# Batch 0 scored in float32 from raw q and k, and every tile of softmax weights split into two float16 halves and transposed by DMA

## The chip, the cores and the metric

The kernel runs on one core of a Trainium2 chip. The metric is the device time of one execution in microseconds, the median over runs. Engines are named as the profile names them: PE is TensorE (PEld its weight loads), DVE VectorE, ACT ScalarE, POOL GpSimd, SP the engine whose queue issues every DMA here.

## The reference

Three parts follow each other. The first is attention with a hash mask: 2 batches, 8 heads, 768 positions, head dimension 64.

```python
q_bits = (q @ proj > 0); k_bits = (k @ proj > 0)      # proj: 64 x 6
mask = bucket(q_bits)[..., :, None] == bucket(k_bits)[..., None, :]
scores = np.where(mask, (q @ k.T) / 8, -1e9)
attn = np.exp(scores - scores.max(-1, keepdims=True))
x = (attn / (attn.sum(-1, keepdims=True) + 1e-9)) @ v
```

Then `x` (1536 tokens x 512) passes a feed-forward layer with softplus, `(max(h,0) + log1p(exp(-|h|))) @ w_out` with `h = x @ w_in` (512 to 2048 to 512), and a gated layer, `(silu(x @ w_gate) * (x @ w_val)) @ w_out2` (512 to 1536 to 512). The feed-forward weights arrive as 64-bit floats and are turned into 32-bit ones, and then into pairs of 16-bit ones, on the chip.

## The kernel before

Precision comes from pairs: a float32 operand is scaled by a power of two, rounded to float16 (`hi`), and the remainder is kept as a second float16 (`lo`). A product of two such operands takes two or three float16 matmuls.

The work is cut into four chunks: batch 0 first half and second half of the query rows, batch 1 first and second half. A chunk has 8 heads of 3 tiles of 128 query rows each, so 24 tiles; a tile is a row block of 128 queries against all 768 keys. For each head the kernel loads k, v, q (`load_kv`, `load_q`), sums their squares and turns the sums into powers of two (`scales`), splits q and k into `natq` and `natk`, transposes these by DMA into `q` and `k` (`query_side`, `key_side`), copies the high half to the other 64 partitions, and lets `planes` make the mask rows: matmuls with the projection give the hash signs, which are written as plus or minus a large constant into rows 0 to 63 of the second operand. So each tile's score is four float16 matmuls of 384 columns (`qk`, L776), in which a mask mismatch comes out as a huge negative number. v is split in `value_side`.

In `units_of` a tile then runs: `qk` on PE; `mx` on DVE (L787), which copies the scores to SBUF, clamps them and takes the row maximum, and a second small DVE instruction (L792) that turns the maximum into the bias of the exponential; `ex` on ACT (L797). From there the kind of the tile decides. Kind F (the 24 tiles of the first half of batch 0): six PE transposes in float32 (L831), an ACT or DVE copy of the result to SBUF (L862), and six float32 matmuls with raw v (L870). Kind D (the other 72 tiles): a high half on ACT, POOL or DVE (L804, L812), a low half on POOL or DVE (L817), one DMA transpose of both (L823), and 18 float16 matmuls with the split v (L854). After the third tile the sums are inverted and the head's output is scaled into `xn`; after eight heads `x_tile` splits and transposes a chunk's rows into `xy`, and `ffn1` and later `ffn2` run on it.

The order of all instructions on all engines is written by a planner (`Order`) while the kernel is built: each step has an urgency, one or more ways (engine, cost, function, and a handicap in us from `BV`), and rings of buffers. Among the steps that can start earliest on an engine, the one of lowest urgency is taken; among ways, the one with the earliest end plus handicap. The engines then run their instructions in that order. Rings that matter here: `E` 3, `P` 2, `PT` 2, `z` (PSUM) 2, `f` (PSUM) 2, `k` 5, `q` 3. All DMAs go through SP's queue in order.

```python
KINDS = ("FFF", "DDD", "DDD", "DDD")          # kinds of a chunk's three tiles
s = ways(u + U["lo"], [("G", gps(S) + 0.05, lo(nc.gpsimd)), ("W", dve(S), lo(nc.vector), BV["lo"])], [s], uses=[E, P])
s = step(u, "D", (1.72, 1.9), tr, [s], takes=[PT], uses=[P], line="tr")
```

The order of visits: batch 0 first halves of heads 0 to 7, then second halves (k of three heads is loaded and split again, because the ring holds five), then batch 1. Beside batch 0 the 16 pieces of the first feed-forward layer's weights are converted on DVE, ACT and POOL (L394 to L448); beside the second half of batch 0 `ffn1` of chunk 0 starts. The gate weights wait until attention has left its buffers.

Of the kernel before, what the change touches and what calls it, by code (L numbers as in the profile page):

```python
# [31 lines left out]

class Step:
# [17 lines left out]
class Order:  # L51
# [8 lines left out]
    SLACK = 0.1077  # L60
# [123 lines left out]
def tile_hash_attention__softplus_ffn__silu_glu(  # L184
# [54 lines left out]
    BV = dict(tf=1.0, th=1.091, hi=2.161, lo=0.772, slo=0.117, wlo=-0.43, bits=0.477, meas=0.564, cv=-0.593, ca=0.872)  # L239
    U = dict(vl=0, tp=-2.89, th=-2, tl=-2, w2=53.21, qp=-7.63, kp=-4.93, kv=3.56, f1=0, y=40, ev=-9.89, ex=3.56, hi=-7.89, lo=2.67, gw=423.98, x=2.84)  # L240
# [22 lines left out]
    KINDS = ("FFF", "DDD", "DDD", "DDD")  # L263
    SPLIT = 3
    RINGS = {
# [41 lines left out]
    nc.vector.memset(ones, 1.0)  # L307

# [10 lines left out]
    nc.vector.tensor_scalar_mul(half_amp, amp, 0.5)  # L319
    floors = small(3)  # L320
# [8 lines left out]
    ones_mat = const.tile([128, 128], F32, name="ones_mat")  # L329
    nc.vector.memset(ones_mat, 1.0)  # L330
# [179 lines left out]
    praw = const.tile([128, NB], F32, name="praw")  # L510

    pm = small()

    def load_proj():
        for r in range(2):
            nc.sync.dma_start(out=praw[64 * r:64 * r + 64], in_=proj)
        for i in range(2):
            for w in range(2):
                nc.gpsimd.memset(pj[i][w], 0.0)

    def prep_proj():
# [12 lines left out]
        for w in range(2):  # L534
            nc.vector.tensor_copy(pj[1][w][:, 0:32], pj[0][w][:, 32:64])
            nc.vector.tensor_copy(pj[1][w][:, 32:64], pj[0][w][:, 0:32])

# [28 lines left out]
    def planes(u, i, n, src, dst, after, takes, uses):  # L566

        ps = [Slot("f") for _ in range(n)]

        def products(x, f):  # L570
            def go():
                new(ps_f, [128, 512], F32, f)
                for w in (1, 0):
# [9 lines left out]
        def bits(x, f):  # L583
            def go():
                nc.vector.tensor_scalar(
                    dst()[0:64, x * HS:(x + 1) * HS], f.t[0:64, 0:HS], thr[0:64, i:i + 1],
                    amp[0:64, i:i + 1], op0=ALU.is_gt, op1=ALU.mult,
                )
            return go

        def signs(x, f):
            def go():
                new(att, [64, HS], F16, hb[x])
                nc.scalar.activation(hb[x].t, f.t[0:64, 0:HS], AF.Sign, bias=low[0:64, i:i + 1])
            return go

        def offset(x):
            def go():
                nc.gpsimd.tensor_scalar(
                    dst()[0:64, x * HS:(x + 1) * HS], hb[x].t, half_amp[0:64, i:i + 1],  # L600
                    half_amp[0:64, i:i + 1], op0=ALU.mult, op1=ALU.add,
# [7 lines left out]
        for x, f in enumerate(ps):  # L609
            s = step(u, "E", pe(2 * HS), products(x, f), after, takes=[f], uses=uses)  # L610
# [25 lines left out]
    def scales(b, h, u, kv, ld_kv, qr, ld_q):  # L636
# [20 lines left out]
        def inverse():  # L657
            for i, c in enumerate((QK_SC, -QK_SC)):
                nc.vector.tensor_scalar(
                    inv[:, i:i + 1], e[:, 0:1], e[:, 1:2], c, op0=ALU.mult, op1=ALU.mult  # L660
                )
        ms = [
            ways(u, [("A", act(n) + 0.15, measure_a(i)), ("V", stt(n) - 0.07, measure_v(i), BV["meas"])],
# [10 lines left out]
    def key_side(b, h, u, hs, raw, ld, proj_ready):  # L674
# [28 lines left out]
        cp = ways(u, [("W", dve(NT * 128, 4), copy_v, BV["cv"]), ("A", act(NT * 128), copy_a, BV["ca"]),  # L703
# [4 lines left out]
    def value_side(u, hs, raw, ld, after=()):  # L708
# [9 lines left out]
        return dict(v=vs, v_ready=split(u, NT * D, parts, [g], [raw, vs]))  # L718

    def query_side(b, h, half, u, hs, raw, ld, proj_ready):  # L720
# [28 lines left out]
        cp = ways(u, [("W", dve(CN, 4), copy_v, BV["cv"]), ("A", act(CN), copy_a, BV["ca"]),  # L749
# [9 lines left out]
    def units_of(b, h, half, due, hs, kd, qd):  # L759

        c = 2 * b + half
        kinds = KINDS[c]
# [4 lines left out]
        for t in range(HT):  # L767
# [3 lines left out]
            def qk(t=t, z=z):  # L771
                a = new(ps_z, [128, 2, 512], F32, z)
                ts = slice(t * 128, (t + 1) * 128)
                for w in range(2):
# [6 lines left out]
            def mx(t=t, z=z, st=st, E=E):  # L781


                if t == 0:
                    new(att, [128, 2, HT], F32, sums)
                a = new(att, [128, 4], F32, st)
                nc.vector.tensor_scalar(  # L787
# [87 lines left out]
            s = step(u, "E", pe(4 * HS), qk, kd["ready"] + qd["ready"], takes=[z], uses=[kd["k"], qd["q"]],  # L875
# [469 lines left out]
```

## Time and profile before

| | us |
|---|---|
| median of 3 runs | 885.31 (883.08 to 885.72) |
| the profiled execution | 884.34 |
| span in its profile | 882.5 |
| PE busy | 779.3 (88%) |
| DVE busy | 584.9 (66%) |
| ACT busy | 460.3 (52%) |
| POOL busy | 407.7 (46%) |
| mean granted clock of PE | 0.957 |

The span is the time from the first to the last instruction of the profiled execution; 1.8 us of its time lie around it. A PE that is shown busy is not a PE at its peak, since matmuls overlap each other.

### The profile page before, as it was taken

The page shows a single profiled execution, that of the slowest core. Times are in us where ns is not written, and L with a number is a line of the kernel's source. Part 1 is how long each engine was busy: PE and PEld are TensorE (multiplying, and loading weights), DVE is VectorE, ACT ScalarE, POOL GpSimd, SP SyncE. Part 2 cuts the span into 40 slices and gives each one's busy share as a digit, 9 for nine tenths or more (in the row PEclk, how much of TensorE's full clock was granted, in tenths as well). Part 3 has the DMA queues.
Part 4 walks back from the last instruction along what each step waited for, and adds up shares of the span by engine and source line. Part 5 has one row for each costly group of instructions (what it writes and reads, how often), then busy time and mean ns, then how long its engine had stood idle before and what let it go on. Part 6 is the DMA issues. An engine that isn't in the chain of part 4 may idle for free.

```text
span 882.5 us, 14634 instructions
## 1 busy us (share of the span) xinstructions
PE 779.3 (88%) x5462; PEld 505.3 (57%) x5462; DVE 584.9 (66%) x1157; ACT 460.3 (52%) x847; POOL 407.7 (46%) x430
## 2 busy tenths in 40 slices
PE   3787776877889886779999999899999999999998
PEld 1565654444445553445566666555576676677666
DVE  4798888789989899999667799968911311220320
ACT  4666667668567688767568548624411211211220
POOL 2345346877578788877348418512311210210220
PEclk9988998889879998899999999999999999999999
DMA  6445457946668787857793541342200000000000
GB/s 186 124 146 167 112 131 172 189 100 149 117 135 162 159 139 146 151 98 135 120 157 70 185 161 40 127 160 96 96 12 25 1 9 28 1 1 36 1 1 36
DMA packets 195048, 90.05 MB, mean 102 GB/s; under 512 B 156640, under 2 KB 181664, under 8 KB 194976
## 3 DMA queue, kind: packets, MB, share of 16 engines
q1 hardware_dynamic: 194976, 89.11, 43.0%
q8 instruction: 43, 0.70, 0.3%
q14 instruction: 29, 0.24, 0.1%
HBM read 47.35 MB, written 3.15 MB: 57 GB/s over the span
## 4 chain that ended last, share of the span: by engine, by line
PE 49%; DVE 22%; DMA 10%; POOL 7%; issue 6%; ACT 3%; SPq 1%; DVEq 0%; POOLq 0%; ACTq 0%
PE z L1020 8%; PE z L1022 8%; PE z L1021 8%; DMA PT<-P 4%; PE f L1183 4%; PE f L1181 4%; PE f L1182 4%; DVE E L787 3%; DVE fr L1061 2%; DMA q<-natq 2%; POOL P L817 2%; DVE fr L1049 2%; PE z L776 2%; DVE w32b L399 1%; PE y L1020 1%
## 5 line engine op out<-in xcount | busy, mean ns | idle before, releaser
L1149 DVE SCALAR_TENSOR_TENSOR sg<-z,smalls,sg 128x384 f32<-128x384 f32 x96 | 59.2, 616 | 176.9 <-ACT sg L1143 175.4
L1158 POOL TENSOR_TENSOR sT<-sg,sT 128x384 fp32r<-128x384 f32 x48 | 51.8, 1080 | 217.0 <-ACT sT L1155 211.1
L797 ACT ACTIVATE E<-E,st,smalls 128x768 f32<-128x768 f32 x96 | 98.1, 1022 | 28.0 <-DVE st L792 25.8
L776 PE MATMUL z<-k,q 128*128 128x384 f16 x384 | 87.6, 359 | 15.7 <-DVE E L787 15.4
L787 DVE TENSOR_SCALAR_CACHE_REDUCE E<-z 128x768 f32<-128x768 f32 x96 | 91.2, 950 | 9.4 <-POOL P L817 5.3
L817 POOL TENSOR_TENSOR P<-E,P 128x768 f16<-128x768 f32 x51 | 87.0, 1708 | 12.7 <-ACT P L804 9.8
L1075 POOL TENSOR_TENSOR g<-fr,g 128x384 f16<-128x384 f32 x64 | 73.6, 1154 | 16.7 <-ACT g L1066 13.1
L1020 PE MATMUL f<-xy,w1h 128*128 128x384 f16 x192 | 65.8, 343 | 10.7 <-DVE fr L1049 9.1
L854 PE MATMUL pv<-v,PT 128*128 128x64 f16 x1296 | 52.4, 197 | 19.1 <-DMA PT<-P 18.4
L854 PEld LDWEIGHTS <-PT 128*128 128x128 f16 x1296 | 47.6, 101 | 34.5 <-DMA PT<-P 27.4
L1021 PE MATMUL f<-xy,w1h 128*128 128x384 f16 x192 | 65.6, 342 | 0.0
L1022 PE MATMUL f<-xy,w1l 128*128 128x384 f16 x192 | 65.4, 341 | 0.0
L1020 PE MATMUL z<-xy,wgh 128*128 128x384 f16 x192 | 62.6, 326 | 0.7 <-DVE sg L1149 0.7
L1020 PE MATMUL z<-xy,wvh 128*128 128x384 f16 x192 | 62.6, 326 | 0.0
L1021 PE MATMUL z<-xy,wvh 128*128 128x384 f16 x192 | 62.6, 326 | 0.0
L1022 PE MATMUL z<-xy,wvl 128*128 128x384 f16 x192 | 62.6, 326 | 0.0
L1022 PE MATMUL z<-xy,wgl 128*128 128x384 f16 x192 | 62.6, 326 | 0.0
L1021 PE MATMUL z<-xy,wgh 128*128 128x384 f16 x192 | 62.6, 326 | 0.0
L776 PEld LDWEIGHTS <-q 128*128 128x128 f16 x384 | 36.3, 106 | 45.5 <-issue 24.5
L1143 ACT ACTIVATE sg<-z,smalls 128x384 f32<-128x384 f32 x48 | 27.8, 580 | 63.6 <-PE z L1022 63.5
L1061 DVE SCALAR_TENSOR_TENSOR fr<-fa,smalls,fr 128x384 f32<-128x384 f32 x64 | 55.4, 869 | 7.8 <-ACT fa L1058 5.4
L1155 ACT ACTIVATE sT<-sg 128x384 fp32r<-128x384 f32 x48 | 25.1, 522 | 61.8 <-DVE sg L1149 61.6
(189 smaller groups left out, 2032.0 us busy)
## 6 DMA issues: line engine op xcount, KB each, us to landing
raw64a<-in_moe_w_in_dram SPq DMA_DIRECT2D x16, 512.0 KB, 4.6
raw64a<-in_moe_w_out_dram SPq DMA_DIRECT2D x16, 512.0 KB, 5.0
raw64b<-in_moe_w_gate_dram SPq DMA_DIRECT2D x12, 512.0 KB, 4.3
raw64b<-in_moe_w_val_dram SPq DMA_DIRECT2D x12, 512.0 KB, 4.9
raw64b<-in_moe_w_out_dram SPq DMA_DIRECT2D x12, 512.0 KB, 4.3
rawk<-in_k_dram SPq DMA_DIRECT2D x19, 192.0 KB, 2.7
rawv<-in_v_dram SPq DMA_DIRECT2D x19, 192.0 KB, 3.3
rawq<-in_q_dram SPq DMA_DIRECT2D x16, 192.0 KB, 3.0
```

What stands on the lines that cost most here:

```text
L776: nc.tensor.matmul(a[:, x, 0:HS], lhsT=qd["q"].t[:, w, ts], rhs=kd["k"].t[:, w, x * HS:(x + 1) * HS], start=(w == 0), stop=(w == 1),)
L787: nc.vector.tensor_scalar(new(att, [128, 2, HS], F32, E), z.t[:, :, 0:HS], MASK_FLOOR, None, op0=ALU.max, op1=ALU.max, accum_out=a[:, 0:1],)
L797: nc.scalar.activation(E.t, E.t, AF.Exp, bias=st.t[:, 1:2], scale=hs["inv"][:, 0:1], accum_out=sums.t[:, 0, t:t + 1],)
L817: return lambda: eng.tensor_tensor(P.t[:, 1, :], E.t.rearrange("p a b -> p (a b)"), P.t[:, 0, :], op=ALU.subtract)
L854: nc.tensor.matmul(pv.t[:, t, :], lhsT=PT.t[:, w, kk, :], rhs=values.t[:, kk, c0:c0 + D], start=(kk == 0 and w == 0 and c0 == 0), stop=(kk ...
L1020: nc.tensor.matmul(ps, lhsT=wh, rhs=xh, start=first, stop=False)
L1021: nc.tensor.matmul(ps, lhsT=wh, rhs=xl, start=False, stop=False)
L1022: nc.tensor.matmul(ps, lhsT=wl, rhs=xh, start=False, stop=last)
L1061: nc.vector.scalar_tensor_tensor(out=fr.t, in0=fa.t, scalar=sc[b]["sg"], in1=fr.t, op0=ALU.mult, op1=ALU.add)
L1075: return lambda: eng.tensor_tensor(g.t[:, 1], fr.t, g.t[:, 0], op=ALU.subtract)
L1149: return lambda: nc.vector.scalar_tensor_tensor(out=sg.t, in0=z.t[:, j, 0:CN], scalar=gvs[b, "gv"[j]][:, gi:gi + 1], in1=sg.t, op0=ALU.mul ...
L1158: return lambda: eng.tensor_tensor(sT.t[:, 1, :], sg.t, sT.t[:, 0, :].bitcast(F32), op=ALU.subtract)
```

## The change

All four chunks become kind D, so the PE transposes, the copies and the float32 products with v of the first half go, and its weights are split and transposed by DMA as the others are; v of batch 0 is split for both halves. In batch 0 (`PLAIN`), q and k are no longer measured, split or DMA-transposed: PE transposes them in float32 (`key_plain`, `query_plain`), ACT or DVE copies the result out of PSUM, `planes` uses one float32 matmul where it used two float16 ones, and writes its rows as float32 into partitions 64 to 127. A score tile is then two float32 matmuls (`qk`), `mx` takes a minimum of the negated score, which is the exponential's bias as it stands, so L792 goes there. In batch 1, L792 may run on ACT as well, and the ReLU of `ffn1` too. The planner's handicaps, urgencies and pacing numbers are new throughout.

```diff
-    SLACK = 0.1077
+    SLACK = 0.1067
-    BV = dict(tf=1.0, th=1.091, hi=2.161, lo=0.772, slo=0.117, wlo=-0.43, bits=0.477, meas=0.564, cv=-0.593, ca=0.872)
-    U = dict(vl=0, tp=-2.89, th=-2, tl=-2, w2=53.21, qp=-7.63, kp=-4.93, kv=3.56, f1=0, y=40, ev=-9.89, ex=3.56, hi=-7.89, lo=2.67, gw=423.98, x=2.84)
+    BV = dict(ck=1.33, re=1.809, st=-2.461, tf=0.612, th=1.593, hi=1.28, lo=5.114, slo=0.343, wlo=0.612, bits=-0.971, meas=1.909, cv=-0.593, ca=0.592)
+    U = dict(st=1.53, vl=-3.48, tp=-22.23, th=-9.5, tl=-1.48, w2=59.9, qp=6.21, kp=1.44, kv=3.56, f1=0.25, y=40, ev=-10.18, ex=2.67, hi=-7.32, lo=2.67, gw=302.78, x=2.18)
-    KINDS = ("FFF", "DDD", "DDD", "DDD")
+    KINDS = (("DDD",), ("DDD",), ("DDD",), ("DDD",))
+    PLAIN = (True, False)
...
+                if plain:
+                    nc.tensor.matmul(
+                        f.t[:, 0:HS], lhsT=pjf, rhs=src()[:, x * HS:(x + 1) * HS], start=True, stop=True
+                    )
+                    return
...
+        if PLAIN[b]:
+            s = ways(u, [("A", act(n) + 0.15, measure_a(2)), ("W", stt(n) + 0.14, measure_v(2), BV["meas"])],
+                     [ld_kv[1]], uses=[kv[1]])
+            s, bank_ = total(u, m[:, 2:3], 1, [s])
...
+    def key_plain(u, raw, ld, proj_ready):
...
+            for t in range(NT):
+                nc.tensor.transpose(
+                    a[0:64, t // HT, t % HT * 128:(t % HT + 1) * 128], raw[0].t[:, t * D:(t + 1) * D], ident
+                )
...
+        s = step(u, "E", 6 * 0.14, turn, [ld[0]], takes=[T, kk], uses=[raw[0]], line="tk")
+        s = ways(u, [("A", act(S) - 0.05, copy(nc.scalar.copy)), ("V", dve(S) + 0.07, copy(nc.vector.tensor_copy), BV["ck"])],
+                 [s], uses=[T, kk])
+        pl = planes(u + U["kp"], 0, 2, lambda: plain(kk)[0:64], lambda: plain(kk), [s, proj_ready], [], [kk], True)
...
+    def query_plain(half, u, raw, ld, proj_ready):
...
+        s = step(u, "E", 3 * 0.14, turn, [ld], takes=[T, qq], uses=[raw], line="tq")
+        s = ways(u, [("A", act(CN), copy_a), ("V", dve(CN) + 0.13, copy_v, BV["ck"])], [s], uses=[T, qq])
...
+                if PLAIN[b]:
+                    for x in range(2):
+                        nc.tensor.matmul(
+                            a[:, x, 0:HS], lhsT=plain(qd["q"])[:, ts], rhs=plain(kd["k"])[:, x * HS:(x + 1) * HS],
+                            start=True, stop=True,
+                        )
+                    return
...
+                if PLAIN[b]:
+                    nc.vector.tensor_scalar(
+                        new(att, [128, 2, HS], F32, E), z.t[:, :, 0:HS], PLAIN_TOP, None,
+                        op0=ALU.min, op1=ALU.min, accum_out=a[:, 1:2],
+                    )
+                    return
...
+            if not PLAIN[b]:
+                s = ways(u + U["st"], [("V", 0.21, base_v), ("A", 0.37, base_a, BV["st"])], [s], uses=[st], line="st")
...
-            r = step(U["f1"], "V", stt(CN) + 0.07, relu, [a, g_ready], takes=[fr], uses=[f])
+            r = ways(U["f1"], [("V", stt(CN) + 0.08, relu), ("A", act(CN) + 0.04, relu_a, BV["re"])], [a, g_ready], takes=[fr], uses=[f])
...
-    T0, GAP, LEAD, W1_GAP, W2_GAP = 12, 2.611, 14.38, 5.974, 6.601
+    T0, GAP, LEAD, W1_GAP, W2_GAP = 12, 2.65, 15.295, 4.228, 9.175
```

## Rows read from the trace of the kernel before

**Rows 1.** Stretches: length, busy PE, PEld, DVE, ACT, POOL (count), clock, DMA share, GB/s.
```profile
0.00:20.00 20.00, 5.80 (x18) 3.13 (x19) 10.30 (x58) 10.12 (x24) 5.27 (x16) 1.00 0.60 177
20.00:140.00 120.00, 94.63 (x595) 70.89 (x593) 100.86 (x243) 78.97 (x149) 50.90 (x62) 0.91 0.51 142
140.00:270.00 130.00, 101.45 (x807) 59.17 (x806) 113.57 (x216) 88.45 (x167) 96.34 (x92) 0.87 0.67 141
...
458.00:592.00 134.00, 130.03 (x860) 79.50 (x858) 111.35 (x164) 81.98 (x149) 66.65 (x65) 0.99 0.42 128
592.00:882.00 290.00, 286.29 (x1589) 193.66 (x1586) 86.12 (x125) 67.57 (x116) 51.82 (x48) 1.00 0.07 26
```

**Rows 2.** The chain of work by line, 20 to 140 us.
```profile
by line: issue 13.8%; DMA k<-natk 8.7%; PE z L831 6.7%; PE pv L870 6.4%; PE z L776 6.2%; DVE E L787 6.1%; DMA q<-natq 4.9%; DMA rawq<-in_q_dram 4.7%; PE f L574 4.0%; ACT E L797 3.8%; ACT PT L862 2.5%; ACT hb L594 2.4%; DMA rawk<-in_k_dram 2
```

**Rows 3.** The chain of work by line, 140 to 270 us.
```profile
by line: issue 10.4%; DMA q<-natq 9.9%; POOL P L817 6.5%; DMA PT<-P 5.5%; DVE E L787 4.5%; DVE fr L1061 4.1%; DVE w2l L448 3.3%; DVE fr L1049 3.0%; DVE w32a L405 3.0%; DMA xy<-xp 2.9%; PE y L1020 2.6%; POOL P L812 2.6%; POOL k L599 2.4%; PE
```

**Rows 4.** Groups on VectorE, 0 to 270 us: busy us, mean ns, idle before.
```profile
L792 DVE TENSOR_SCALAR st<-st,smalls 128x1 f32<-128x1 f32 x48 | 10.3, 214 | 1.7
...
L557 DVE SCALAR_TENSOR_TENSOR natk<-rawk,smalls,natk 128x384 f16<-128x384 f32 x9 | 7.1, 791 | 1.5 <-ACT natk L545 1.0 <-POOL natk L553 0.4
...
L741 DVE COPY q<-q 64x384 f16<-64x384 f16 x12 | 4.5, 375 | 1.4 <-DMA q<-natq 1.1
...
L647 DVE SCALAR_TENSOR_TENSOR junk<-rawq 128x384 bf16<-128x384 f32 x5 | 4.2, 843 | 0.1
...
L695 DVE COPY k<-k 64x768 f16<-64x768 f16 x10 | 3.8, 383 | 1.5 <-DMA k<-natk 1.2
L557 DVE SCALAR_TENSOR_TENSOR natq<-rawq,smalls,natq 128x192 f16<-128x192 f32 x9 | 3.7, 410 | 0.0
...
L585 DVE TENSOR_SCALAR k<-f,smalls 64x384 f16<-64x384 f32 x4 | 2.6, 657 | 0.0
```

**Rows 5.** Groups on ScalarE, 0 to 270 us.
```profile
L594 ACT ACTIVATE hb<-f,smalls 64x384 f16<-64x384 f32 x36 | 20.0, 571 | 18.0 <-PE f L574 15.5 <-POOL natq L553 2.0
L862 ACT COPY PT<-z 128x768 f32<-128x768 f32 x24 | 18.9, 790 | 7.5 <-PE z L831 7.1
L804 ACT CAST P<-E 128x768 f16<-128x768 f32 x15 | 12.4, 825 | 6.1 <-DMA PT<-P 6.0
```

**Rows 6.** Groups on GpSimd, 0 to 270 us.
```profile
L817 POOL TENSOR_TENSOR P<-E,P 128x768 f16<-128x768 f32 x19 | 33.2, 1751 | 4.9 <-ACT P L804 4.4
L599 POOL TENSOR_SCALAR k<-hb,smalls 64x384 f16<-64x384 f16 x20 | 20.3, 1018 | 9.3 <-ACT hb L594 9.1
```

**Rows 7.** Timeline, the start: start us, us, engine, line, op, operands, count.
```profile
4.60 0.52 ACT L644 ACTIVATE junk<-rawk 128x384 bf16<-128x384 f32 x1 [2.54 <-DMA rawk<-in_k_dram]
...
7.01 0.52 ACT L644 ACTIVATE junk<-rawq 128x384 bf16<-128x384 f32 x1 [1.15 <-DMA rawq<-in_q_dram]
...
25.31 0.96 DVE L787 TENSOR_SCALAR_CACHE_REDUCE E<-z 128x768 f32<-128x768 f32 x1
```

**Rows 8.** Timeline of TensorE inside the first half of batch 0.
```profile
50.30 0.83 PE L831 MATMUL z<-ident,E 128*128 128x128 f32 x6
...
51.45 0.81 PE L776 MATMUL z<-k,q 128*128 128x384 f16 x4
...
52.09 1.53 PE L870 MATMUL pv<-rawv,PT 128*128 128x64 f32 x12
```

**Rows 9.** One record each of two of these, 0 to 270 us: ns min/median/max.
```profile
L776 PE MATMUL z<-k,q x192: 322/326/528, 18.4 to 264.5; 128*128 128x384 f16 x192
...
L831 PE MATMUL z<-ident,E x144: 272/273/477, 27.9 to 138.4; 128*128 128x128 f32 x144
```

**Rows 10.** The same for one tile of the second half.
```profile
204.11 0.70 PE L854 MATMUL pv<-v,PT 128*128 128x64 f16 x18
```

**Rows 11.** DMA transposes into tile PT, 0 to 270 us.
```profile
DMA to landing us min/median/max: 3.7/4.0/7.2
```

**Rows 12.** DMA transposes out of tile natk, 0 to 270 us.
```profile
DMA to landing us min/median/max: 2.5/2.9/6.8
```

More of the change, by code (lines that the diff above doesn't have):

```diff
@@ L319, in tile_hash_attention__softplus_ffn__silu_glu @@
     nc.vector.tensor_scalar_mul(half_amp, amp, 0.5)
+    pthr, plow, pamp, phalf = small(2), small(2), small(2), small(2)
+    nc.vector.tensor_scalar_mul(pthr, thr, PLAIN_TINY / TINY)
+    nc.vector.tensor_scalar_mul(plow, thr, -PLAIN_TINY / TINY)
+    for i in range(2):
+        nc.vector.tensor_scalar_mul(pamp[:, i:i + 1], amp[:, i:i + 1], (1, -1)[i] * PLAIN_C / MASK_C)
+    nc.vector.tensor_scalar_mul(phalf, pamp, 0.5)
     floors = small(3)
@@ L510, in tile_hash_attention__softplus_ffn__silu_glu @@
     praw = const.tile([128, NB], F32, name="praw")
+    pjf = const.tile([64, 128], F32, name="pjf")
     pm = small()
@@ L592, in go @@
             def go():
-                new(att, [64, HS], F16, hb[x])
-                nc.scalar.activation(hb[x].t, f.t[0:64, 0:HS], AF.Sign, bias=low[0:64, i:i + 1])
+                new(att, [128, HS], F16, hb[x])
+                nc.scalar.activation(hb[x].t[r], f.t[r, 0:HS], AF.Sign, bias=low_[r, i:i + 1])
             return go
@@ L609, in planes @@
         for x, f in enumerate(ps):
-            s = step(u, "E", pe(2 * HS), products(x, f), after, takes=[f], uses=uses)
+            s = step(u, "E", pe(4 * HS if plain else 2 * HS), products(x, f), after, takes=[f], uses=uses)
             b = ways(u, [("V", dve(HS) + 0.14, bits(x, f), BV["bits"]), ("A", act(HS), signs(x, f))], [s],
@@ L895, in units_of @@
                 s = step(u + U["tl"], "V", dve(S), lo_t, [s], uses=[T, PT], line="tl")
-            s = pvs = step(u, "E", 1.8 if full else pe(18 * 64), apply_f if full else apply,
+            s = pvs = step(u, "E", 1.6 if full else pe(18 * 64), apply_f if full else apply,
                            [s, v_ready] + ([pvs] if t else []),
@@ L902, in ev2a @@
             sm = sums.t
-            if full:
+            if PLAIN[b]:
                 nc.gpsimd.tensor_scalar(
-                    sm[:, 1], sm[:, 0], 1e-9 * 2.718281828459045 ** E_SHIFT, 1.0, op0=ALU.add, op1=ALU.mult,
+                    sm[:, 1], sm[:, 0], 1e-9, 1.0 if full else hs["x"][:, 2:3], op0=ALU.add, op1=ALU.mult,
                 )
@@ L924, in units_of @@
         u += U["ev"]
-        a = step(u, "G", 0.15, ev2a, [x], uses=[sums])
+        a = step(u, "G", 0.25, ev2a, [x], uses=[sums])
         a = step(u, "V", 0.17, ev2b, [a], uses=[sums])
@@ L1052, in relu, with relu_a @@
                 )
+            def relu_a(gi=gi, f=f, fr=fr):
+                nc.scalar.activation(
+                    new(gpool, [128, CN], F32, fr), f.t[:, 0:CN], AF.Relu, scale=sc[b]["invg"][:, gi:gi + 1]
+                )
             def ex(fa=fa):
```

100 lines of the change are left out of this document (78 added, 22 removed).

## The prediction

> **What bounds the kernel now.** I read the table of stretches first [rows 1]. From 592 us on PE is busy 286.3 of 290 us at full clock, and from 458 on 130.0 of 134: there PE sets the time, and the change touches nothing that runs there except the order. Before 458 no engine is full. From 20 to 140 us (the first half of batch 0, 24 tiles) DVE is busy 100.9 of 120 us and PE 94.6, at a clock of 0.91; from 140 to 270 (the second half, 24 tiles, with `ffn1` of chunk 0 beside it) DVE 113.6 of 130, PE 101.5, POOL 96.3, at a clock of 0.87. So what the change does to batch 0 is worth what it takes from, or gives to, the first 270 us, and every microsecond by which attention ends earlier is one at the end only if PE has by then done the same share of the feed-forward work.
>
> The chain of work says who is late in these two stretches [rows 2, 3]. No line has more than a tenth apart from "issue". What stands out is DMA: the transposes of k and q, `k<-natk` and `q<-natq`, hold 8.7% and 4.9% of the first stretch and `q<-natq` 9.9% of the second: 0.136 x 120 + 0.099 x 130 = 29 us. The transposes of the weights, `PT<-P`, hold 5.5% of the second, 7 us. The reader is to see a kernel that loses its time to many hand-overs, with DVE the fullest engine and no single wall.
>
> **The start.** k has landed by 4.60 us and q by 7.01 (that is when ACT measures them), but the first row maximum runs at 25.31 [rows 7]. After the change nothing is measured or split before the first score: PE transposes, a copy (0.79 like the PT copy, [rows 5]), the mask rows, two matmuls. Six transposes take 0.83 us, a score pair about 1.5 (below), a sign 0.57 and an offset 1.02 [rows 5, 6, 8]; at the low clock of a start PE's part doubles. That is about 7 + 3 + 3 + 1 = 14 us, some 11 us earlier. Weight work can stand in front of it in DVE's queue, and DVE can gain only the time that it stood idle: 20 less 10.3 in the first stretch [rows 1]. Bounds 0 and -11; I take half, **-5**.
>
> **Chain of k and q.** A k costs a high half, a low half, a DMA transpose of 2.9 us (median, up to 6.8, [rows 12]) and a copy of 0.38 [rows 4]; it becomes 0.83 of PE and 0.79 of copy. Of the 2.9 us some 1.6 remain as other waits, so of the 29 us on the chain 29 x (1 - 1.6/2.9) = 13 go: **-13**. Bounds: 0, if the same tiles then wait for a busy PE or ACT, and -29.
>
> **DVE.** Gone in batch 0: L792 10.3, the low halves of k and q 7.1 + 3.7, the copies to the other partitions 4.5 + 3.8, the measuring of q that ran there 4.2: 33.6 [rows 4], and 32 with the items taken off that are batch 1's already. Added: three more splits of v, at 0.79 like those of k, 2.4 us. The copies out of PSUM and the new halves have ways on ACT and POOL: 8 + 3 of k at 0.79, 16 of q at 0.57, 24 high halves at 0.83 [rows 5] make 38 us on ACT, where the PT copies' 18.9 and the measuring and splitting of q and k go; 24 low halves at 1.75 make 42 us on POOL [rows 6], where the splitting of q and k goes. The new handicaps send low halves to POOL (DVE 5.1 us behind instead of 0.8) and the sign bits to DVE (1.0 ahead instead of 0.5 behind): up to 36 at 0.66, 24 us back onto DVE [rows 4], for 0.57 + 1.02 each off ACT and POOL. Three low halves leave DVE, 4 us. So DVE loses 32 - 2.4 - 24 + 4 = 10 us, in stretches where it is busy for 0.84 and 0.87 of the time; I put nine tenths of it on the path: **-9**. Bounds 0 and -10.
>
> **PE.** A tile of the first half loses six transposes (0.83) and the product of 1.53, and gains one of 0.70 [rows 8, 10]. The price of a float32 score isn't in the trace; the bounds are. A float16 score of four matmuls takes 0.81, the last one's 0.33 included, so (0.81 - 0.33)/3 = 0.16 us per 384 columns, 0.42 ns a column [rows 8, 9]. The float32 product has twelve records for six matmuls, so a float32 matmul is two records. The float32 transposes give (0.83 - 0.27)/5 = 0.11 us per 128 columns, 0.87 ns a column; the product (1.53 - 0.27)/11 = 0.115 us per 64 columns, 1.8 ns, though each of its records also loads weights. So four records of 384 columns take 0.65 us (nothing added), 1.34, or 2.8. The transposes are the nearest in width; I take 0.87 ns and add 0.17 for the end, 1.5. Then a tile of the first half costs 2.2 instead of 3.17, -0.97 x 24 = -23; of the second +0.7 x 24 = +17. The mask rows: 38 halves of 384 columns at +0.35, +13. The transposes of q and k: 11 x 6 + 16 x 3 = 114 at 0.11, +12.5. Sum +19: about -7 in the first half, where 24 of the 38 and 72 of the 114 lie, and +26 in the second. PE has 28.5 us idle there; with a third on the path **+8**. Bounds 0 and +26.
>
> The Trainium skill, "Perfetto Trace Analysis", section "Engine Utilization", gives half the array's rate for a float32 low or high pass. By it a record of 384 columns would be 0.32 us and a score 1.3, as an estimate; the sum would be 2 us smaller on PE. No row here shows a wide float32 matmul.
>
> **The weights by DMA in the first half.** 24 transposes, landing in 4.0 us (3.7 to 7.2, [rows 11]). Those of the second half, about as many, hold 7 us of the chain [rows 3], so 24 in the first: **+7**. Bounds 0 and +20 (rival below). On SP's queue they replace 11 + 16 transposes of k and q. The Trainium skill, "VectorE: DVE Perf Modes", section "The three transpose paths", speaks against this step: 390 ns for a 128 x 128 block on TensorE and 1309 ns by DMA. By it the twelve blocks of a tile would take 15.7 us by DMA, as an estimate, and 24 tiles 377 us; the trace lands all twelve in 4.0, so this has no chance of its own and I go by the trace.
>
> **Batch 1 and the rest.** New handicaps and pacing reorder everything; L792 and the ReLU may leave DVE there and the sign bits come to it. I price that at 0, with 5 us either way.
>
> **The sum.** 884.3 - 5 - 13 - 9 + 8 + 7 = 872.3 us for an execution like the profiled one. The median of the runs shown is 1.0 above it, so I predict **873 us**.
>
> **Rivals.**
> - *The weights' ring sets the pace of the first half* (slower). A P buffer is held from the high half to the landing: 0.83 + 1.75 + 4.0 = 6.6 us, two buffers, 3.3 us a tile at best, and any wait on POOL or on SP behind a 512 KB weight load adds to it. In the second half tiles come every 130/24 = 5.4 us, in the first every 120/24 = 5.0. If the first half fell to 5.8, it costs +20 in place of +7, the gains from k, q and DVE are kept in the second half alone (-6), and the start is lost behind the ring: 884 - 6 + 20 + 8 = 906, and with part of the start kept 890 to 906. For it: POOL's low halves already stand idle 4.4 us for the high half and ACT's high halves 6.0 for `PT<-P` [rows 5, 6]. Against: POOL is busy for only 50.9 of 120 us there [rows 1]. It decides once a first-half tile takes over 5.0 us. Chance 0.19.
> - *PE fills in the second half.* All 26 us land on the path: 872 + 18 = 890, less what a denser PE gains in clock, (1 - 0.87) x 101 = 13 us at most; 880 to 892. Chance 0.13.
> - *The hand-overs go entirely.* Start -11, chain -29, DVE -10, PE 0 as the clock rises, +7: 841 at its bound; 845 to 862 as a case. Chance 0.20.
> - *A float32 score costs 2.8 us.* +2 a tile x 48 = +96, mask rows +40: PE alone then needs over 300 us for batch 0, 920 and more. Against it: the rate comes from 64-column products that load weights each time. Chance 0.03.
>
> **How the numbers follow.** My forecast (862 to 880) has 0.45. The range for eight in ten reaches from **852** to **896**: it leaves out about half of the fast rival, the upper part of the slow one and the last. A measurement of this kernel tells no change apart below about 0.3%, 882.7 to 888.0. Faster: 0.45 + 0.20 less a tail, **0.63**; same, most of the full-PE rival, **0.11**; slower **0.26**.
>
> **What would show it.** Right: the first row maximum before 20 us; no DMA line of q or k on the chain; the 48th row maximum by 255 us or so; scores in float32 at 1.3 to 1.5 us a tile; the clock over 0.91 in batch 0; and the last stretch at 290 us as now. Wrong: first-half tiles over 5.0 us with ACT and POOL waiting for `PT<-P`; PE at its full in the second half while `ffn1` of chunk 0 comes out later; or attention earlier but a longer stretch between its end and the gated layer.

## The result and the profile after

| | before | after |
|---|---|---|
| median | 885.72 us (15 runs, 879.5 to 889.47) | 876.05 us (15 runs, 869.36 to 883.8) |
| the profiled execution, its span | 884.34, 882.5 us | 875.31, 873.5 us |
| PE busy, PE idle (span less busy) | 779.3, 103.2 us | 799.8, 73.7 us |
| DVE, ACT, POOL busy | 584.9, 460.3, 407.7 us | 549.0, 450.8, 437.4 us |
| mean granted clock of PE | 0.957 | 0.958 |

After to before is 0.9886, 95% interval 0.9858 to 0.9914: 1.1% faster. Executions over 1.5% above the fastest of their kernel, two of the 15 after, are not in the ratio, so it isn't exactly the quotient of the medians. The forecast was 873 us in a range of 852 to 896. The ledger of PE already says what kind of gain it is: PE has 20.5 us more to do and stands idle 29.5 us less, 9.0 us between them, the whole difference of the spans.

The stretches after, which answer to [rows 1]:

```profile
0.00:20.00 20.00, 14.67 (x41) 8.44 (x42) 11.12 (x56) 8.55 (x17) 3.27 (x14) 1.00 0.65 206
20.00:140.00 120.00, 96.79 (x687) 56.61 (x686) 97.08 (x193) 69.85 (x124) 81.34 (x61) 0.92 0.80 179
140.00:270.00 130.00, 108.79 (x808) 63.10 (x807) 106.73 (x174) 88.97 (x177) 98.75 (x85) 0.83 0.79 164
458.00:592.00 134.00, 130.21 (x855) 79.86 (x853) 110.00 (x163) 77.47 (x144) 60.93 (x59) 1.00 0.38 121
592.00:873.00 281.00, 277.30 (x1533) 188.28 (x1531) 82.53 (x117) 64.45 (x112) 51.82 (x48) 1.00 0.08 27
```

From 0 to 270 us PE is busy 220.3 us where it was 201.9, and from 20 to 270 us DVE 203.8 where it was 214.4. From 20 to 140 us POOL is busy 81 us where it was 51, and DMA's share is 0.80 where it was 0.51.

The chain of work by line of the kernel after, 20 to 140 us and then 140 to 270 us, against [rows 2, 3]:

```profile
by line: DMA PT<-P 39.1%; PE z L869 13.6%; POOL P L929 8.8%; issue 5.2%; PE f L602 5.2%; DVE w32a L419 5.1%; DMA raw64a<-in_moe_w_in_dram 4.6%; PE pv L966 4.6%; DVE E L888 3.3%; DVE w32a L413 2.0%; PE z L774 1.2%; DVE q L618 1.2%; PE f L799
...
by line: DMA PT<-P 11.4%; issue 8.6%; PE z L869 8.0%; POOL P L929 6.4%; DVE w32a L419 4.8%; POOL g L1194 4.4%; DVE fr L1180 3.5%; PE pv L966 3.4%; PE f L1134 3.2%; PE f L602 3.1%; DVE w2l L462 3.0%; DVE E L888 2.9%; PE f L1135 2.9%; PE f L1
```

No transpose of k or q is left in it. In their place the transposes of the weights hold 0.391 x 120 + 0.114 x 130 = 62 us; the score matmuls (13.6% of the first stretch) and the low halves on POOL (8.8%) come next. Two groups of the page of the kernel after show the same hand-over from the other side, a high half on ACT that waits for a P buffer and a low half on POOL that waits for the high half (busy us, mean ns, idle before by releaser):

```profile
L929 POOL TENSOR_TENSOR P<-E,P 128x768 f16<-128x768 f32 x96 | 172.7, 1802 | 46.3 <-ACT P L916 40.4
...
L916 ACT CAST P<-E 128x768 f16<-128x768 f32 x66 | 54.6, 827 | 39.9 <-DMA PT<-P 36.8
```

The start, the 25th row maximum and a float32 score at full clock, from the timeline of the kernel after:

```profile
14.38 0.69 DVE L618 TENSOR_SCALAR q<-f,smalls 64x384 f32<-64x384 f32 x1 [0.42 <-PE f L602]
...
14.91 1.48 PE L774 MATMUL z<-ident,rawk 128*64 128x128 f32 x6
...
16.54 1.64 PE L602 MATMUL f<-k,pjf 64*128 64x384 f32 x2
...
18.11 2.93 PE L869 MATMUL z<-k,q 128*128 128x384 f32 x4
...
21.08 0.96 DVE L888 TENSOR_SCALAR_CACHE_REDUCE E<-z 128x768 f32<-128x768 f32 x1 [1.52 <-PE z L869]
...
119.05 0.96 DVE L888 TENSOR_SCALAR_CACHE_REDUCE E<-z 128x768 f32<-128x768 f32 x1 [0.23 <-POOL P L929]
...
227.51 1.45 PE L869 MATMUL z<-k,q 128*128 128x384 f32 x4
```

The first row maximum comes 4.2 us earlier than in [rows 7]. A score tile of four records is 1.45 us at full clock and 2.93 us at the start, half the rate, although the profile's clock figure for 0 to 20 us is 1.00.

The row maxima by tile E, with first and last start: all of the kernel before (L787), then batch 0 (L888) and batch 1 (L893) of the kernel after. Behind them stand the last one of batch 0 and the first of batch 1 before, from its timeline:

```profile
L787 DVE TENSOR_SCALAR_CACHE_REDUCE E<-z x96: 927/948/960, 25.3 to 457.2; 128x768 f32<-128x768 f32 x96
```

```profile
L888 DVE TENSOR_SCALAR_CACHE_REDUCE E<-z x48: 922/956/958, 21.1 to 234.7; 128x768 f32<-128x768 f32 x48
L893 DVE TENSOR_SCALAR_CACHE_REDUCE E<-z x48: 923/957/960, 259.5 to 448.9; 128x768 f32<-128x768 f32 x48
```

```profile
266.82 0.96 DVE L787 TENSOR_SCALAR_CACHE_REDUCE E<-z 128x768 f32<-128x768 f32 x1
...
272.92 0.94 DVE L787 TENSOR_SCALAR_CACHE_REDUCE E<-z 128x768 f32<-128x768 f32 x1
```

The first matmuls of the gated layer, before and after:

```profile
L1020 PE MATMUL z<-xy,wgh x192: 323/326/336, 592.5 to 851.9; 128*128 128x384 f16 x192
```

```profile
L1134 PE MATMUL z<-xy,wgh x192: 322/326/336, 583.5 to 842.9; 128*128 128x384 f16 x192
```

Here is the riddle. Batch 0's last row maximum was at 266.8 us before and is at 234.7: attention is 32 us ahead. Then no row maximum starts for 25 us, where the gap between the batches was 6 us, and the last one starts at 448.9 instead of 457.2 (called attention's end from here on), only 8 us ahead; the gated layer begins at 583.5 instead of 592.5, and takes 290.0 us to the end in both. The second thing to see is `ffn1`. Its second layer in chunk 0 starts, by tile y, first in the kernel before and then in the one after:

```profile
L1020 PE MATMUL y<-g,w2h x128: 322/326/528, 230.5 to 455.2; 128*128 128x384 f16 x128
```

```profile
L1134 PE MATMUL y<-g,w2h x128: 322/326/524, 269.4 to 449.1; 128*128 128x384 f16 x128
```

So while attention is 32 us ahead, the feed-forward work that PE does beside it is 39 us behind. From 235 to 260 us, which is between the two batches in the kernel after and still in batch 0 in the one before, PE was busy 20.06 of 25 us at a clock of 0.80 before; it is busy 14.24 at 0.56 after, with DVE and POOL nearly full (22.48 and 23.27 us):

```profile
235.00:260.00 25.00, 20.06 (x174) 12.00 (x173) 21.89 (x57) 15.83 (x29) 17.09 (x17) 0.80 0.72 137
```

```profile
235.00:260.00 25.00, 14.24 (x114) 8.41 (x114) 22.48 (x34) 16.29 (x32) 23.27 (x21) 0.56 0.97 206
```

### The profile page after: what moved, and what is told of

It is laid out like the page before. It is cut to its first block, busy times and chain, and to the rows that moved or that the text cites. A ratio compares the mean times of both kernels' runs of the same rounds, so it can differ in the third digit from the quotient of the medians.

```text
span 873.5 us, 14618 instructions
## 1 busy us (share of the span) xinstructions
PE 799.8 (92%) x5576; PEld 503.4 (58%) x5576; DVE 549.0 (63%) x1000; ACT 450.8 (52%) x857; POOL 437.4 (50%) x408
## 4 chain that ended last, share of the span: by engine, by line
PE 55%; DVE 18%; DMA 13%; POOL 6%; issue 5%; ACT 2%; SPq 0%; DVEq 0%; POOLq 0%; ACTq 0%
DMA PT<-P 10%; PE z L1134 8%; PE z L1135 8%; PE z L1136 8%; PE f L1300 4%; PE f L1302 4%; PE f L1301 4%; PE z L869 3%; PE pv L966 3%; POOL P L929 3%; DVE fr L1180 2%; PE f L602 2%; PE f L1134 2%; PE z L876 2%; PE f L1135 2%
## 5 line engine op out<-in xcount | busy, mean ns | idle before, releaser
L929 POOL TENSOR_TENSOR P<-E,P 128x768 f16<-128x768 f32 x96 | 172.7, 1802 | 46.3 <-ACT P L916 40.4
L966 PEld LDWEIGHTS <-PT 128*128 128x128 f16 x1728 | 64.0, 101 | 57.1 <-DMA PT<-P 45.0
L966 PE MATMUL pv<-v,PT 128*128 128x64 f16 x1728 | 70.3, 198 | 29.0 <-DMA PT<-P 27.8
L869 PE MATMUL z<-k,q 128*128 128x384 f32 x192 | 84.3, 570 | 7.5 <-DVE E L888 7.2
L1194 POOL TENSOR_TENSOR g<-fr,g 128x384 f16<-128x384 f32 x64 | 71.8, 1127 | 13.2 <-ACT g L1185 8.1
L916 ACT CAST P<-E 128x768 f16<-128x768 f32 x66 | 54.6, 827 | 39.9 <-DMA PT<-P 36.8
L1134 PE MATMUL f<-xy,w1h 128*128 128x384 f16 x192 | 64.7, 337 | 8.1 <-DVE fr L1163 4.9
L1135 PE MATMUL f<-xy,w1h 128*128 128x384 f16 x192 | 64.7, 337 | 0.0
L869 PEld LDWEIGHTS z<-k,q 128*128 128x128 f32 x192 | 37.7, 216 | 37.2 <-issue 15.3
L1300 PE MATMUL f<-woh,sT 128*128 128x512 f32 x144 | 56.6, 393 | 0.0
```

Of the source, the lines that this page charges most:

```text
L869: nc.tensor.matmul(a[:, x, 0:HS], lhsT=plain(qd["q"])[:, ts], rhs=plain(kd["k"])[:, x * HS:(x + 1) * HS], start=True, stop=True,)
L916: nc.scalar.copy(P.t[:, 0, :], E.t.rearrange("p a b -> p (a b)"))
L929: return lambda: eng.tensor_tensor(P.t[:, 1, :], E.t.rearrange("p a b -> p (a b)"), P.t[:, 0, :], op=ALU.subtract)
L966: nc.tensor.matmul(pv.t[:, t, :], lhsT=PT.t[:, w, kk, :], rhs=values.t[:, kk, c0:c0 + D], start=(kk == 0 and w == 0 and c0 == 0), stop=(kk ...
L1134: nc.tensor.matmul(ps, lhsT=wh, rhs=xh, start=first, stop=False)
L1135: nc.tensor.matmul(ps, lhsT=wh, rhs=xl, start=False, stop=False)
```

## The experiments

Three theories stood at the start, and the expectations call them by letters: the gain is in the path of q and k, which the float32 scores shorten (A); in the new planner numbers (B); or in the weights by DMA (C). That the two halves of the change pay only together was in none of them. Ratios are to the kernel before, which ran again beside each group of kernels (its medians are 884.6 to 887.9 us), with 95% intervals; across groups, compare the ratios and not the medians. Spans, busy times and stretches are those of the one profiled execution of each kernel. A table of all runs stands at the end of this section.

**e4_new_numbers_only.** Both halves undone, the new numbers and the added ways kept.

```diff
-    KINDS = (("DDD",), ("DDD",), ("DDD",), ("DDD",))
+    KINDS = (("FFF",), ("DDD",), ("DDD",), ("DDD",))
-    PLAIN = (True, False)
+    PLAIN = (False, False)
```

> The kernel before in its structure (float16 scores, PE transposes of the first half's weights) with the new numbers and the added ways for L792 and the ReLU. Theory A: no gain, 882 to 890 us, ratio 0.996 to 1.005. Theory B: 872 to 880.

Measured: 878.58 us, 0.9936 (0.9891 to 0.9981). The numbers alone make the old work 0.6% faster, theory B's range and more than half of the 1.1% that the whole change gives. What the new work adds to that, 0.9886/0.9936 or half a per cent, is no larger than the two intervals together leave open.

**e3_old_numbers.** The changed work with the numbers of before, those that only the added ways have (`ck`, `re`, `st`) kept. A part of the edit, which sets all of `SLACK`, `BV`, `U` and the pacing back:

```diff
-    T0, GAP, LEAD, W1_GAP, W2_GAP = 12, 2.65, 15.295, 4.228, 9.175
+    T0, GAP, LEAD, W1_GAP, W2_GAP = 12, 2.611, 14.38, 5.974, 6.601
...
-    BV = dict(... lo=5.114, ... bits=-0.971, meas=1.909, ...)
+    BV = dict(... lo=0.772, ... bits=0.477, meas=0.564, ...)
```

> The changed kernel with the handicaps, urgencies and pacing of the kernel before (the three handicaps that are new keep their values). Theory A: most of the gain stays, 872 to 880 us. Theory B (the new numbers are the gain): 884 to 892, ratio near 1.00.

Measured: 894.35 us, 1.0093 (1.0062 to 1.0124), though batch 0's attention ends at 232.4 us, as early as in the kernel after. This is above the ranges of both theories, on B's side. The new work under the old numbers is slower than before; the numbers are worth 0.9886/1.0093, 2.1%, on the new work and 0.6% on the old.

**e1_weights_by_dma** and **e2_f32_scores.** One half each, under the new numbers: in the first all weights go by DMA and q and k of batch 0 are split as before; in the second the scores are float32 and the first half's weights are transposed by PE as before.

```diff
-    PLAIN = (True, False)
+    PLAIN = (False, False)
```

```diff
-    KINDS = (("DDD",), ("DDD",), ("DDD",), ("DDD",))
+    KINDS = (("FFF",), ("DDD",), ("DDD",), ("DDD",))
```

> Batch 0 keeps its float16 scores with measured, split and DMA-transposed q and k; only the first half's weights go by DMA, under the new planner numbers. If the gain comes from the path of q and k (theory A), this has lost it and pays for the added transposes: 884 to 896 us, ratio 0.998 to 1.012. If the weights by DMA are the gain (theory C): 872 to 880, ratio 0.985 to 0.994. If the new numbers are the gain (theory B): also below 880.

> Batch 0 is scored in float32 from raw q and k, the first half's weights stay with the float32 PE transposes and products, under the new numbers. Theory A: 872 to 881 us, ratio 0.985 to 0.995, and the chain of the first 140 us without DMA lines of q, k or PT. Theory C: the scores bring nothing and PE is loaded by 30 us more, 886 or more.

Measured: 923.34 us, 1.0422 (1.0353 to 1.0492), and 913.1 us, 1.0294 (1.0229 to 1.0358). Each half by itself loses 3 to 4%, and both together gain. The first is outside every theory's range (A had 884 to 896, B and C under 880); the second is above A's range, in the one for scores that bring nothing. None of the three theories is left as it stood. Against e4, which has neither, PE's ledger says where: the DMA half has PE busy for 12.3 us less and idle for 55.2 us more; the float32 half has it busy for 49.4 us more and idle for 14.3 us less; the two together 16.1 us more and 19.3 us less. The one stretch to look at in the DMA half is 20 to 140 us:

```profile
20.00:140.00 120.00, 70.91 (x557) 39.56 (x556) 104.00 (x207) 80.77 (x165) 89.28 (x79) 0.69 0.88 198
```

DVE, ACT and POOL are all fuller than in the kernel after, since they split q and k as well as the weights; PE has 71 us of work and a clock of 0.69. The float32 half does the opposite: PE keeps the transposes and float32 products of the weights [rows 8] and takes the float32 scores too, 833.1 us in all. The halves are two sides of one exchange: one moves the weights off PE onto the other engines and DMA, the other moves q and k off those and onto PE. Neither half was run with numbers of its own, so how much of these losses belongs to the half, and how much to an order that doesn't suit it, is not shown; e13 below wins back 1.8 of the first one's 4.2 points by the order alone.

**e9_slack_control.** One number back, as a measure of what a reshuffled order alone does.

```diff
-    SLACK = 0.1067
+    SLACK = 0.1077
```

> The changed kernel with one planner number put back (SLACK 0.1077 instead of 0.1067), no other difference. It tells how far a reordering that means nothing moves the time: if under 3 us, differences of 5 us between structures can be read as effects of the structure; if 8 us or more, the new numbers and the structure can't be told apart by single kernels.

Measured: 876.79 us, 0.9913 (0.9872 to 0.9954), not told apart from the kernel after, and by the medians under the 3 us that the expectation set. It is one small reshuffle; e5 and e7 below change the order by more, and the time with it.

**e6_score_dose.** The first of the two score matmuls of each float32 tile runs twice, with the same result: 96 records more, at 0.32 us 31 us of PE.

```diff
-                    for x in range(2):
+                    for x in (0, 0, 1):
```

> The changed kernel with the first of the two float32 score matmuls of each batch 0 tile issued twice, the planner not told: 48 more float32 matmuls of 384 columns, some 31 us more of PE at full clock, which is what the float32 scores added. If that PE time lies on the path, +20 to +31 us, 896 to 907; if it is hidden behind DVE, POOL and DMA and paid back by the clock, under +8, below 884. My prediction had a third on the path, so about +10.

Measured: 878.75 us, 0.9927 (0.9903 to 0.9952), 0.4% above the kernel after. Its stretches:

```profile
20.00:140.00 120.00, 107.64 (x704) 64.45 (x703) 92.78 (x185) 65.39 (x116) 74.27 (x58) 0.94 0.76 175
140.00:270.00 130.00, 111.67 (x862) 67.33 (x860) 106.75 (x176) 89.62 (x176) 100.19 (x85) 0.91 0.80 163
```

The 31 us make PE's busy time only 17.0 us longer (816.8) and its idle time 11.5 us shorter. The granted clock is higher: its mean over an execution is 0.973 in the median of ten, against 0.962 in 15 of the kernel after. By the ratios 3.6 of the 31 us reach the end, give or take 3.3, and 5.5 in the profiled executions: in batch 0 most of PE's time is hidden, as the expectation's second branch had it.

**e5_p_ring.** A third P buffer for the hand-over that the chain shows, in the room of one xp buffer.

```diff
-        "st": 4, "E": 3, "P": 2, "PT": 2, "xp": 2, "xn": 2,
+        "st": 4, "E": 3, "P": 3, "PT": 2, "xp": 1, "xn": 2,
```

> The changed kernel with three P buffers instead of two (and one xp buffer instead of two, to make room). If the P ring and the landing of its transposes set the pace of the whole (PT<-P is 39% of the chain from 20 to 140 us), the time falls by 5 us or more, ratio to before 0.983 or less. If attention in batch 0 is ahead of what the end needs anyway, the first 24 tiles come sooner and the end stays within 3 us of the changed kernel's 876.

The row maxima of this kernel, by tile E:

```profile
L888 DVE TENSOR_SCALAR_CACHE_REDUCE E<-z x48: 921/957/959, 21.6 to 199.3; 128x768 f32<-128x768 f32 x48
L893 DVE TENSOR_SCALAR_CACHE_REDUCE E<-z x48: 926/946/958, 210.3 to 400.3; 128x768 f32<-128x768 f32 x48
```

The ring did set attention's pace: batch 0 ends 35 us and all of attention 49 us earlier than in the kernel after. And the time is 907.38 us, 1.026 (1.021 to 1.031), 31 us worse. (That one xp buffer is gone is part of the edit; it wasn't tried alone.) Neither branch of the expectation saw a loss. Attention's end is not what sets this kernel's.

**e7_early_batch1.** Batch 1's first two heads get 60 us more urgency, to close the hole at 235 to 260 us.

```diff
-        u = due - LEAD
+        u = due - LEAD - (60 if b and h < 2 else 0)
```

> The changed kernel with the preparation of the first two heads of batch 1 made 60 us more urgent. The row maxima of batch 0 end at 234.7 us and those of batch 1 begin at 259.5. If that hole is what gave the gain of batch 0 back, the hole closes to under 8 us and the time falls by 8 to 16, 860 to 868. If PE's backlog of feed-forward work decides, the hole closes and the end moves by less than 4.

Measured: 913.54 us, 1.0322 (1.0261 to 1.0384). The hole is closed (row maxima from 240.8 straight to 246.8), attention's end hardly moves (451.8), and 37 us are lost, where the expectation had a gain or under 4 us either way. Closing it this way costs more than the hole did.

These two gave a new theory. The planner writes each engine's order out beforehand, with the matmuls of `ffn1` as filler behind all attention (urgency 1000 and more, against dues of 12 for the first tile and 2.65 more for each, some 264 for the last). The expectations call `ffn1` the gelu layer and a tile an attention unit. In PE's order the first layer of chunk 0 is complete after the products with v of 36 of the 96 attention tiles in the kernel before, 48 in the one after, 73 in e5 and 64 in e7. By the theory a late place leaves gaps that nothing fills, and the matmuls come back at the end, where PE is full. The last four kernels test it: chunk 0's matmuls, of both of its layers, get urgency 150 in the kernel after, in e5, in e7 and in e1. The rival is that DVE, ACT and POOL are what is full there, so that filler put ahead only pushes attention back.

```diff
-                s = step(due + 1e3, "E", pe(3 * KD * CN / PARTS) - ...
+                s = step((due + 1e3 if c else 150), "E", pe(3 * KD * CN / PARTS) - ...
...
-                s = step(due + 1e3 + U["y"], "E", pe(3 * per * CN), mm,
+                s = step((due + 1e3 + U["y"] if c else 150), "E", pe(3 * per * CN), mm,
```

> The kernel after, with the matmuls of the gelu layer's first chunk (both of its layers) given the urgency 150 in place of 1000 and more, so that PE's order takes them ahead of batch 1's attention; nothing else is edited. In PE's order the first layer of that chunk was already complete at the 48th of 96 attention units and stays there; the second layer moves from the 64th unit to the 57th. Filler theory (the end is set by how much of the gelu layer PE has done before attention ends, so a late place in its order costs idle PE): the place hardly moves, so 870 to 878. Engine theory (VectorE, ScalarE and GpSimd are what is full at 240 to 340 us, so matmuls put ahead only push attention back): 876 to 890.

> e5_p_ring (a third P buffer, 907 us, attention done at 400 us) with the same urgency 150 for the gelu layer's first chunk. In PE's order its first layer is then complete at the 54th attention unit in place of the 73rd. Filler theory: e5 lost its attention lead because PE stood idle 30 of the 100 us between 240 and 340 with these matmuls queued behind batch 1; with them back PE's idle time there falls to 15 us or less, and the time to 865 to 885. Engine theory: VectorE was busy 92 and GpSimd 87 of those 100 us already; attention moves back by as much as the layer gains, 900 to 912.

> e7_early_batch1 (batch 1's first two heads 60 us more urgent, 913.5 us) with the urgency 150 for the gelu layer's first chunk. Its first layer is then complete at the 48th attention unit, as in the kernel after, in place of the 64th. Filler theory: the loss of e7 was the gelu layer's place and not the earlier heads, so most of the 37 us come back: 875 to 888. Engine theory: the earlier heads take VectorE and GpSimd from the layer's evictions whatever PE's order is: 905 to 918.

> e1_weights_by_dma (all weights by DMA, the scores of batch 0 from 16-bit halves as before; 923 us) with the urgency 150 for the gelu layer's first chunk. Its first layer is then complete at the 50th attention unit in place of the 68th. Filler theory: what the DMA half cost alone was mostly this place: 885 to 900. Engine theory: without the float32 scores VectorE and PE are the slower ones through batch 0 (clock 0.74), and nothing comes back: 915 to 928.

Measured: 883.85, 892.1, 890.85 and 907.8 us; ratios 0.9948 (0.991 to 0.9987), 1.0078 (1.0034 to 1.0123), 1.0054 (1.0018 to 1.0089) and 1.0244 (1.0182 to 1.0306). The three that had been thrown back get 1.8 points of 3.7 lost against the kernel after (e5), 2.7 of 4.4 (e7) and 1.8 of 5.4 (e1). The stretch from 240 to 340 us in the kernel after, in e7 and in e12:

```profile
240.00:340.00 100.00, 85.19 (x728) 49.75 (x726) 82.81 (x168) 71.39 (x150) 78.19 (x77) 0.84 0.83 160
```

```profile
240.00:340.00 100.00, 72.28 (x677) 43.91 (x676) 82.49 (x163) 77.57 (x161) 85.13 (x81) 0.80 0.86 165
```

```profile
240.00:340.00 100.00, 83.40 (x744) 50.98 (x742) 79.82 (x153) 72.75 (x150) 76.52 (x71) 0.90 0.73 139
```

PE gets its work back there (72.3 to 83.4 us), and DVE and POOL are less busy than before the edit, not more; in e11 PE's idle time in this stretch falls from 30.4 to 16.2 us, just above the 15 that the expectation had. The place of the filler is shown to be a cause, of a third to six tenths of each loss. It is not all of it: the three times lie between what the two theories gave, and the traces show both at work. The edit shortens the time from attention's end to the gated layer by 48.7, 39.2 and 43.5 us in e11, e12 and e13, and it makes attention end 40.1, 7.8 and 31.1 us later, as the rival has it. So less work on DVE and POOL in that stretch is in part attention that was pushed out of it. In the kernel after, where the place was already at tile 48, the same edit costs 0.6% (the intervals just touch), in the rival's range, with attention's end 4.8 us later. e12 begins chunk 0's second layer at 259.9 us, before the kernel after does, and is 1.7% slower than it: attention ends 10.7 us later, and its gated layer takes 6.2 us longer. Why e11 still needs 30 us more between attention's end and the gated layer than the kernel after stays open.

All kernels, from their results and profiles (us). "First y" is the start of chunk 0's second layer; "place" is the number of attention tiles whose product with v stands before the end of chunk 0's first layer in PE's order; "att end" is the start of the last row maximum, and "to gate" the time from there to the first matmul of the gated layer:

```
kernel                median   ratio    PE busy  PE idle  first y  place  att end  to gate
before                885.72   1        779.3    103.2    230.5    36     457.2    135.3
e4_new_numbers_only   878.58   0.9936   783.7     93.0    239.3    40     449.2    137.3
after                 876.05   0.9886   799.8     73.7    269.4    48     448.9    134.6
e9_slack_control      876.79   0.9913   796.5     78.4    269.1    48     450.5    134.5
e6_score_dose         878.75   0.9927   816.8     62.2    273.9    48     453.5    135.6
e10_after_fill        883.85   0.9948   797.6     81.7    263.4    48     453.7    135.6
e12_early_fill        890.85   1.0054   802.0     86.1    259.9    48     459.6    132.4
e13_dma_fill          907.80   1.0244   762.0    145.1    292.8    50     479.2    137.7
e3_old_numbers        894.35   1.0093   800.2     93.3    298.4    52     455.8    141.5
e11_ring_fill         892.10   1.0078   801.0     94.5    262.3    54     440.4    165.1
e2_f32_scores         913.10   1.0294   833.1     78.7    317.2    60     451.4    169.8
e7_early_batch1       913.54   1.0322   813.6    100.0    333.9    64     451.8    171.6
e1_weights_by_dma     923.34   1.0422   771.4    148.2    345.7    68     448.1    181.2
e5_p_ring             907.38   1.0260   806.3     98.1    337.3    73     400.3    213.8
```

No kernel whose first y comes after 290 us is faster than before; e11 and e12 show that an early one is not enough. The last two columns say more. From the first matmul of the gated layer to the end every kernel takes 290 us (e3 and e12 296), so its end is the sum of the two columns and a constant. Up to a place of 52 the time from attention's end to the gated layer is 132 to 142 us, whatever else differs, and from 54 on it is 165 to 214. So in the kernel after, with 134.6 us, nearly all of the gain is attention's end, 8.3 of 9.0 us; and in e5 the 49 us of attention were lost to 79 us behind it.

## Why the prediction came out right, and where its reasons did not

The sign, the time and the range held. Taken by its own steps:

**The start.** Forecast -5; it came 4.2 us earlier, at 21.08. The size was right, and the sign of a row maximum before 20 us was missed by 1.1 us. The mask rows of q were written at 15.07 (14.38 + 0.69), but in PE's order transposes and mask rows for further heads stand before the first score, which ran at 18.11 and took 2.93 us.

**The prices on PE.** A float32 score was put at 1.5 us between 0.65 and 2.8; it is 1.45 at full clock. The Trainium skill, "Perfetto Trace Analysis", section "Engine Utilization", gives half the array's output rate for what it calls FP32_LOW_HIGH; taken as the rate of one record, the trace agrees: the records follow each other at (1.45 - 0.486)/3 = 0.32 us for 384 columns, where float16 ones do at 0.16 [rows 8, 9]. The added busy time to 270 us was put at 19 and is 18.4, but that agreement is luck. Before, 19.05 us of PE's time to 270 us went to chunk 0's second layer (tile y), which has hardly begun by then after:

```profile
0.00:270.00 270.00, 19.05 (x102) 1.22 (x2) 1.16 (x2) 0.90 0.60 144
```

```profile
0.00:270.00 270.00, 0.62 (x4) 0.00 (x0) 0.00 (x0) 0.89 0.78 174
```

After, 11.9 us of batch 1's scores and mask rows (L876, L607) lie in it instead. Without these two the rest rose by some 25 us, part of it at a low clock. What reaches the end was put at a third; by e6 it is 3.6 of 31 us, about an eighth, so of the 26 us in the second half some 3 were due and not 8. The clock did not stay over 0.91 in batch 0 as looked for: it is 0.92 in the first stretch and 0.83 in the second.

**DVE.** Put at 10 us less in batch 0; 10.6 measured from 20 to 270 us, with the same reservation on what the window holds. Whether nine tenths of it are on the path can't be read from any run.

**The chain of k and q, and the weights by DMA.** The k and q lines did leave the chain (29 us before). The price of the weights in their place was wrong by far as a line of the chain: +7 was reckoned from the 7 us of [rows 3], and 62 us of `PT<-P` stand there. The mechanism was that of the slow rival, a P buffer held until its transpose lands, with ACT waiting for it; e5 shows it by its 35 us. It did not decide, because it ran at a better pace than the rival's limit of 5.0 us a tile: the 25th row maximum begins at 119.05 us, (119.05 - 21.08)/24 = 4.1 us a tile, so batch 0 was over at 234.7 us where the prediction looked for 255. As to the single transfer, twelve blocks in one go, the Trainium skill, "VectorE: DVE Perf Modes", section "The three transpose paths", has 1309 ns for a block of 128 x 128 by DMA, 15.7 us for the twelve of a tile as an estimate; all twelve land in 3.6 to 8.1 us after, 4.0 in the median. The measurement decides.

**From batch 0 to the end.** This is a step that failed, though the time was met. The prediction said that a microsecond of attention counts only if PE has by then done the same share of the feed-forward work, and it named `ffn1` of chunk 0 coming out later, beside a full PE, as a sign of being wrong. It priced neither, and carried the gains of batch 0 to the end. In batch 0 they were larger than forecast: its last row maximum came 32.1 us earlier, where 12 were looked for; 7.0 of these came with the numbers alone (e4, 259.8 us). Of the 32.1 us, 18.6 went in the gap between the batches (24.7 us against 6.1) and 5.1 in a slower batch 1; 8.3 are left at attention's end. There PE has the same work left as before, 134.6 us against 135.3 to the gated layer: what it did of the feed-forward work moved with attention and not ahead of it. In e4 attention ends at 449.2 us, so what the new work won in batch 0 is gone by attention's end. e5 and e7 show the extreme of it, and e11 to e13 that the place in PE's order is part of the cause.

**The new numbers, priced at 0 with 5 either way.** This is the other step that failed. Alone they give 0.6%, 6 us, about what the bound allowed (e4); but on the new work they are worth 2.1%, and without them the change loses 0.9% (e3). The terms for the work itself sum to -12 in the prediction; with the numbers already in place the work gives 0.9886/0.9936, half a per cent, 4 us, and by the two intervals anything from nothing to 9. So the forecast of 873 was met by luck in good part: about 6 us from a term that was put at nothing and about 4 from terms that were put at 12. The sum also added the two halves as if each stood alone; e1 and e2 show that each alone costs 3 to 4% under these numbers, and that only both together leave PE at 73.7 us of idle time.

Of the rivals, "PE fills in the second half" and "a float32 score costs 2.8 us" fell by the measured 1.45 us, by e6 and by PE's 108.8 us of 130 from 140 to 270 us, "the hand-overs go entirely" by the 62 us on the chain.

## What to carry to other kernels

Where the last stretch is full on one engine, keep that engine's ledger: the work added to it and the idle time taken from it, up to that stretch. A stage that ended 32 us earlier gave 9 us here, and one that ended 49 us earlier lost 31, while the filler that this engine did beside it moved back; so read where the filler stands in the written order before pricing the lead. And where work is exchanged between engines, price the halves together: here either by itself filled one side and starved the other, under numbers that suited both together.

## What the hardware showed that was not expected

More matmuls came with a higher clock: with 31 us of PE work added to batch 0 (e6) the mean granted clock of an execution was 0.967 to 0.977 in ten executions, where it was 0.955 to 0.970 in 15 of the kernel after. One stretch of one profile shows less than it seems to: from 140 to 270 us the clock was 0.91 in e6 and 0.83 in the kernel after, but also 0.88 in e9 and 0.91 in e10, which add no matmuls. The fall itself can be seen in the timeline of TensorE of the kernel after, between the batches:

```profile
232.74 0.33 PE L1134 MATMUL f<-xy,w1h 128*128 128x384 f16 x1
232.91 0.33 PE L1135 MATMUL f<-xy,w1h 128*128 128x384 f16 x1
233.07 0.33 PE L1136 MATMUL f<-xy,w1l 128*128 128x384 f16 x1
236.29 0.38 PE L359 MATMUL f<-smalls 128*128 128x3 f32 x2 [2.90 <-DVE fr L1163]
236.61 0.70 PE L966 MATMUL pv<-v,PT 128*128 128x64 f16 x18
238.57 1.14 PE L966 MATMUL pv<-v,PT 128*128 128x64 f16 x18 [1.26 <-DMA PT<-P]
239.52 0.51 PE L1134 MATMUL f<-xy,w1h 128*128 128x384 f16 x1
239.82 0.53 PE L1135 MATMUL f<-xy,w1h 128*128 128x384 f16 x1
240.14 0.53 PE L1136 MATMUL f<-xy,w1l 128*128 128x384 f16 x1
```

After idle gaps of 2.90 and 1.26 us the same matmul of 384 columns follows its forerunner at 0.32 us, not at 0.16: the lower of the two levels, 1.2 GHz. The filler that followed these gaps cost twice its time. The DMA side held more than expected. With a share of 0.80 from 20 to 140 us the weights' transposes there still land in 4.4 us in the median, where they took 4.0 before [rows 11]:

```profile
DMA to landing us min/median/max: 3.7/4.4/7.4
```
